# Second batch's z loaded earlier and turned in four pieces, unit 1's waiting squares put into feed-forward buffers, and a quarter of each diagonal block filled by a transpose instead of scores

## The chip, the cores and the metric

One core of a Trainium2 chip runs the whole kernel. The metric is the device time of one execution in microseconds (us); smaller is better. The kernel before was timed in 3 runs: 1248.04, 1248.33 and 1249.73 us, median 1248.33 us. The profile comes from one further execution, which has its own time of 1249.53 us.

The engines are called by short names: PE multiplies matrices (PEld is its loading of weights, which overlaps the multiplying), DVE and ACT are the two engines that can read PSUM and do elementwise work here, POOL does elementwise work in SBUF and issues some DMAs, and SP issues the other DMAs, strictly one after the other.

## What is computed

Two layers, one behind the other: a gated attention without softmax, and a feed-forward layer on its result.

```python
# u, v: (8, 3008, 256), z: (8, 3008, 64)
scores = (1/S) * (z @ z.T)              # per batch, S = 3008: symmetric
attn = maximum(scores, 0) ** 2          # symmetric as well
x = u * (attn @ v)
# x: (24064, 256), w_in: (256, 2048), w_out: (2048, 256)
h = x @ w_in
g = h * (1 / (1 + exp(-1.702 * h)))
out = g @ w_out                         # float32
```

The squared scores of a batch form a symmetric 3008 by 3008 matrix, since both factors of the product are the same z.

## The kernel before, in words

**Units and tiles.** A batch has 3008 rows, which are handled as 24 blocks of 128 (`NJ`; the last block has 64 rows, loaded twice). Query columns are taken 512 at a time: these are the *units*, `n` = 0 to 47, six to a batch (`NIS` = 6, `isup = n % 6`). For a unit, the keys are taken in pairs of blocks, `t` = 0 to 11; the pair `t` holds blocks `2t` and `2t+1`. One *score tile* `(n, t)` is made by `scores` (L250): two matmuls of 64 rows by 512 columns, which run side by side in the two halves of PE (L263), into a PSUM tile; a relu by ACT or DVE from PSUM to a float16 tile of 128 x 1024 (L292, L294); and a square in place (L278, L280). With `t // 2 == isup` the tile lies on the diagonal: its four key blocks are the unit's own four query blocks.

**Half of the matrix is transposed, not computed.** From unit 3 on, the tiles below the diagonal (`turned_from`, L186) are not computed: a tile of an earlier unit is transposed by a DMA that SP issues (`turn`, L231, L242) into one of 12 turned tiles `T`. The diagonal tiles are computed in full, in each unit two of them, `t = 2*isup` and `t = 2*isup + 1`. Tiles live in a ring of 14 buffers (`ap_`, `NA`), and `a_left` counts what still has to read one before its buffer is used again. In batch 0 nothing can be taken from a turned tile at first, so units 0 and 1 keep six tiles each outside the ring (`home`, L200): those of unit 0 in the not yet needed `V16[1]`, three of unit 1 in `ZT[1]` and three in `z16`.

**Values and feed-forward.** `values` (L391) multiplies the squares with `v` into four PSUM banks (L403: two matmuls of 64 rows by 256 columns side by side for each 128 x 128 block). At the end of a unit the banks are drained by ACT and DVE (L382, L384), summed and gated with `u` by POOL (L377, L419), transposed by SP (`turn_x`, L318, L325) into `XT` and copied with the halves exchanged into `XS` (`swap_x`, L336). The feed-forward layer takes 512 tokens `m` at a time, three units behind (`LAG`): `hidden` (L486, L493) makes one of 8 hidden tiles, ACT its sigmoid (L500), DVE the product `GT` (L504; 8 buffers, `NG`), and `outs` (L520, L531) multiplies with `w_out`.

**z of the next batch.** `load_z` (L105) is a DMA on POOL's queue into `z16`; `turn_z` (L116) copies all 24 blocks beside themselves on POOL (L118), and then SP transposes all of `z16` into `ZT[b % 2]` in one DMA (L119). `ZT` is the operand of all scores of batch `b`.

**What sets the order.** The order is worked out when the program is built, by a planner in the same file that keeps a clock for each engine (`now`) and adds a fixed cost for each operation (`cost`, L131). `work` (L556 to L577) is the fixed sequence on PE: the value steps `o` of unit `n`, then the output steps `y` of block `n - 3`. Between two steps, whenever a PSUM tile is free in the planner's clock, `filler` (L667) puts in a score tile or a hidden tile, the one that is due sooner. Elementwise operations go to the engine that ends first (`advance`, L152); DMAs of SP wait in `sends` and go out by their due number, lowest first, as soon as the planner's clock says that they are ready. Loads hang on steps of `work` (`at`, L593; L600 to L609): a step `(n, j)` is the first value step of unit `n` with key block `j`, and `hold` (L221) makes POOL wait for the newest square first. For the second batch (b = 1) z is loaded at (3, 8) and turned at (4, 0), later than in the other batches, because unit 1's squares sit in `ZT[1]` and `z16`; for the others at (n0+1, 13) and (n0+2, 13), where n0 is the first unit of the batch before. The filler counts z as there as soon as `turn_z` has been called (L115, L258, L673); it keeps no time for the transpose.

Of the kernel before, what the change touches and what calls it, by code (L numbers as in the profile page):

```python
# [9 lines left out]
F16 = mybir.dt.float16  # L10
P = 128
# [3 lines left out]
def kernel(  # L15
# [10 lines left out]
    AF = mybir.ActivationFunctionType  # L26
    ALU = mybir.AluOpType

    B, S, D = u.shape
    DQK = z.shape[2]  # L30
# [4 lines left out]
    ISUP = 512  # L35
    NIB = ISUP // P
    NIS = (S + ISUP - 1) // ISUP
    NP = NJ // 2
    NTOK = B * S
    TB = 512  # L40
# [4 lines left out]
    LAG = 3  # L45
    RING = (LAG + 1) * TB
    H = P // 2
    assert NTOK % TB == 0 and NJ == NIS * NIB and 2 * DQK == P and 2 * SREM == P and D == 2 * P and TB == ISUP

    CSC = 16.0  # L50
    FSC = CSC * CSC * float(S) * float(S)

    dve, act, pe, sp, pool = nc.vector, nc.scalar, nc.tensor, nc.sync, nc.gpsimd
# [3 lines left out]
    NG = 8  # L57
# [6 lines left out]
    pb = ctx.enter_context(tc.tile_pool(name="pb", bufs=2))  # L64
# [30 lines left out]
    VQ = 4  # L95
    VN = NJ // VQ
# [8 lines left out]
    def load_z(b):  # L105
        rows(b, z, 0, NJ, z16[:, :, 0, :], pool)
# [4 lines left out]
                f0 = e * DFF // 2 + c * D  # L111
                pool.dma_start(W1[e * H:(e + 1) * H, c, :, :], moe_w_in[:, f0:f0 + D].rearrange("(k p) f -> p k f", p=H))

    turned = {0}

    def turn_z(b):  # L116
        turned.add(b)
        pool.tensor_copy(z16[:, :, 1, :], z16[:, :, 0, :])  # L118
        sp.dma_start_transpose(ZT[b % 2], z16.rearrange("p n a d -> p (n a d)"))  # L119

# [7 lines left out]
    now = {"pe": 6.0, "act": 6.0, "dve": 7.0, "pool": 6.0, "sp": 6.0}  # L130
    cost = {  # L131
        ("act", "relu"): 1.03, ("dve", "relu"): 1.23, ("act", "sq"): 1.03, ("dve", "sq"): 0.7,
        ("act", "part"): 0.6, ("dve", "part"): 0.7, ("pool", "add"): 1.1, ("act", "sig"): 1.03, ("dve", "gt"): 1.23, ("pool", "gate"): 1.2,
        ("sp", "turn"): 1.45, ("sp", "turn_x"): 2.6, ("sp", "store"): 0.6, ("sp", "swap"): 1.2,
    }
    BOTH = ("act", "dve")
    FIRST = ("part", "gate", "add")
# [6 lines left out]
    def push(ready, kind, engines, fn):  # L144
        nonlocal pushed
        pushed += 1
        ops.append((ready, pushed, kind, engines, fn))

    def send(ready, kind, due, fn, ok=None):
        sends.append((ready, kind, due, fn, ok))  # L150

    def advance(t):  # L152

        while ops:
            best = None
            for o in ops:
                e = min(o[3], key=lambda x: max(now[x], o[0]) + cost[(x, o[2])])
                key = (max(now[e], o[0]), o[2] not in FIRST, o[2] == "sq", o[1])
                if best is None or key < best[0]:
                    best = key, o, e  # L160
            (start, *_), o, e = best
            if start > t:
                break
            ops.remove(o)
            now[e] = start + cost[(e, o[2])]
            o[4](e, now[e] + T_SEM)
        while now["sp"] <= t:
            can = [o for o in sends if o[0] <= t and (o[4] is None or o[4]())]
            if not can:
                break  # L170
            o = min(can, key=lambda o: (o[2], o[0]))
            sends.remove(o)
            now["sp"] = max(now["sp"], o[0]) + cost[("sp", o[1])]
            o[3](now["sp"])

    def pe_at(rows_, dur):
        if mode[0] != rows_:
            now["pe"] += T_SW
            mode[0] = rows_
        now["pe"] += dur  # L180
        return now["pe"] + T_LAT
# [4 lines left out]
    def turned_from(n, J):  # L186
        return n >= NDIR and J < n % NIS and (n, J) != (NDIR, NDIR - 1)

    def turns(n, t):

        return t // 2 > n % NIS and turned_from(n - n % NIS + t // 2, n % NIS)

    pairs = [(n, t) for n in range(NU) for t in range(NP) if not turned_from(n, t // 2)]
    nxt = 0


    def lend(x, k):
        return x[:, k * 2 * ISUP:(k + 1) * 2 * ISUP].rearrange("p (g c) -> p g c", g=2)

    home = {}  # L200
    for k in range(6):
        home[(0, 6 + k)] = lend(V16[1].rearrange("p n d -> p (n d)"), k)
        home[(1, 6 + k)] = lend(ZT[1].rearrange("p n d -> p (n d)") if k < 3 else z16.rearrange("p n a d -> p (n a d)"), k % 3)
    ring = []
    A, A_at, a_left = {}, {}, {}
    T, T_at, T_left, T_col = {}, {}, {}, {}
# [24 lines left out]
    def turn(n, t, at):  # L231

        b, isup = divmod(n, NIS)
        key = (b * NIS + t // 2, isup)
        if key not in T:
            c = colors.pop(0)
            T_col[key] = c
            T[key] = ptp.tile([P, NIB, NIB, P], F16, name=f"T{c}", tag=f"T{c}")
            T_left[key] = [2, NIB]
        a = A[(n, t)]  # L240
        g0 = (t % 2) * 2
        sp.dma_start_transpose(  # L242
            T[key][:, g0:g0 + 2, :, :].rearrange("p g i r -> p (g i) r"), a.rearrange("p g c -> p (g c)"),
        )
        T_left[key][0] -= 1
        if T_left[key][0] == 0:
            T_at[key] = at + T_DMA
        a_left[(n, t)] -= 1

    def scores(k):  # L250

        nonlocal nxt
        for i in range(k):
            n, t = pairs[nxt]
            nxt += 1
            b, isup = divmod(n, NIS)
            Z = ZT[b % 2]
            assert b in turned  # L258
            p_ = take_ps()
            sc = psA.tile([P, 2, ISUP], F32, name="sc", tag="A")  # L260
            for g in range(2):
                h0 = g * DQK
                pe.matmul(  # L263
                    sc[:, g, :], Z[h0:h0 + DQK, 2 * t + g, :],
                    Z[h0:h0 + DQK, isup * NIB:(isup + 1) * NIB, :],
                    start=True, stop=True,
                )
            if (n, t) in home:
                a = home[(n, t)]
            else:  # L270
                a = pap.tile([P, 2, ISUP], F16, name="ap_", tag="ap_")
                ring.append((n, t))
            A[(n, t)] = a
            a_left[(n, t)] = 2 + turns(n, t)

            def squared(e, at, n=n, t=t, a=a, isup=isup):
                if e == "act":
                    act.activation(a, a, AF.Square, scale=1.0)  # L278
                else:
                    dve.tensor_tensor(a, a, a, ALU.mult)  # L280
                if isup == NIS - 1 and t == NP - 1:
                    pool.memset(a[:, 1, ISUP - SREM:], 0.0)
                    at += 0.5
                A_at[(n, t)] = at
                latest[0] = a
                if turns(n, t):
                    key = (n - isup + t // 2, isup)
                    send(at, "turn", NDIR if n == 1 and (n, t) in home else key[0], lambda at: turn(n, t, at), lambda: key in T or len(colors) > 0)

            def relu(e, at, p_=p_, sc=sc, a=a, squared=squared):  # L290
                if e == "act":
                    act.activation(a, sc, AF.Relu, scale=CSC)  # L292
                else:
                    dve.tensor_scalar(a, sc, 0.0, CSC, ALU.max, ALU.mult)  # L294
                set_ps(p_, at)
                push(at, "sq", BOTH, squared)

            push(pe_at(H, T_SC), "relu", BOTH, relu)

    Os, Ys, GTs, Xs = {}, {}, {}, {}  # L300
    outs_done = 0
# [39 lines left out]
    def squares_of(n, j, ib):  # L341

        J = j // NIB
        if turned_from(n, J):
            return T[(n, J)][:, ib, j % NIB, :]
        return A[(n, j // 2)][:, j % 2, ib * P:(ib + 1) * P]

    def squares_at(n, j):

# [243 lines left out]
    def at(n, j, *fns):  # L593
        def go():
            hold()
            for f in fns:
                f()
        side[(n, j)] = go
# [4 lines left out]
    for b in range(1, B):  # L603
        n0 = (b - 1) * NIS
        late = b == 1
        at(n0 + 1 + 2 * late, 8 if late else 13, lambda b=b: load_z(b))
        at(n0 + 2 + 2 * late, 0 if late else 13, lambda b=b: turn_z(b))
        for q in range(VQ):
            at(n0 + 3 + late + q // 2, (EDGE + late, 12)[q % 2], lambda b=b, q=q: load_v(b, q))  # L609

# [56 lines left out]
    def filler():  # L667

        p_ = ps_free[ps_next % 2]
        if p_ is None or p_ > now["pe"]:  # L670
            return None
        can = []
        if nxt < len(pairs) and pairs[nxt][0] // NIS in turned and min(now["act"], now["dve"]) < now["pe"] + 0.8:  # L673
            old = len(ring) - NA
            if pairs[nxt] in home or old < 0 or not a_left[ring[old]]:
                can.append((urgent(("a",) + pairs[nxt], 3.0), "a"))
        if hnext < len(hids) and hnext - outs_done < NG and now["act"] < now["pe"] + 1.5 and now["dve"] < now["pe"] + 2.0:
            m = hids[hnext][0]
            xt = xt_at[m * TB // 64:(m + 1) * TB // 64]
            if None not in xt and max(xt) <= now["pe"] and (m or work[wi][1] >= LAG or work[wi][0] == "y"):  # L680
                can.append((urgent(("h",) + hids[hnext], 5.0), "h"))
        return min(can, default=None)

# [70 lines left out]
```

## Time and profile before

| what | value |
|---|---|
| median of 3 runs | 1248.33 us |
| profiled execution, its own time | 1249.53 us |
| its span (first to last instruction) | 1247.8 us |
| PE busy, matmuls | 1228.2 us, 18600 instructions |
| DVE, ACT, POOL busy | 937.7, 819.2, 472.9 us |
| SP's transposes of score tiles (L242) | 232 issues |
| transposes of z (L119) | 7 issues, median 4.195 us each on SP |
| copies of z on POOL (L118) | 7, 1454 ns each |
| HBM traffic | 60.29 MB read, 24.64 MB written |

How to read it: an engine's busy time is the union of its instructions. The page has the span in 40 slices, so a stall of a few microseconds shows only in queries with a window. A line such as `L263 PE MATMUL sc<-ZT 64*128 64x512 f16 x688` stands for all 688 matmuls of line 263 that write the tile `sc` from `ZT`, 64 rows by 512 columns. In lists of waits each entry is who waited, at which line, for whose result, the sum, the count and the longest. An arrow in brackets at the end of a line of a timeline tells how long the engine had been idle before it and what ended that. PEclk is the share of the full TensorE clock that the profile's clock rows show as granted in that stretch.

### The profile page before, as it was taken

What the parts mean: (1) busy time and instruction counts of PE and PEld (TensorE: products, weight loads), DVE (VectorE), ACT (ScalarE), POOL (GpSimd) and SP (SyncE); (2) the same over time, 40 slices, a digit from 0 to 9 for tenths busy, and PEclk for the clock granted to TensorE, in tenths of its full rate; (3) what the DMA queues carried; (4) which work ended last, traced back from release to release, by engine and by line L of the source; (5) the groups of instructions that cost most, each with busy time, mean ns of one, the idle gap of its engine ahead of it and who ended that gap; (6) DMA issues with size and microseconds to landing.
All of it is one profiled execution on the core that took longest, in us unless ns stands there. A gap on an engine that the chain in (4) does not pass through costs nothing.

```text
span 1247.8 us, 41921 instructions
## 1 busy us (share of the span) xinstructions
PE 1228.2 (98%) x18600; PEld 1012.1 (81%) x18600; DVE 937.7 (75%) x906; ACT 819.2 (66%) x933; POOL 472.9 (38%) x447
## 2 busy tenths in 40 slices
PE   8898999999999999999999999999999999999998
PEld 6786789989998877888778887788877888778886
DVE  8975877677888778876788768877687776877556
ACT  8765677666767657766667656676566665766444
POOL 5443343432434335343343424343343434322331
PEclk9998999999999999999999999999999999999999
DMA  9998796867987939788399684968659876575211
GB/s 158 176 175 144 142 133 133 149 113 124 135 148 148 147 90 137 145 151 150 85 137 154 131 144 95 134 126 166 131 102 149 158 126 117 113 144 104 67 45 60
DMA packets 442134, 161.74 MB, mean 130 GB/s; under 512 B 351840, under 2 KB 441952, under 8 KB 441952
## 3 DMA queue, kind: packets, MB, share of 16 engines
q1 hardware_dynamic: 390528, 141.62, 60.1%
q0 software_dynamic: 51424, 17.44, 14.5%
q8 instruction: 145, 2.38, 0.8%
q14 instruction: 37, 0.30, 0.1%
HBM read 60.29 MB, written 24.64 MB: 68 GB/s over the span
## 4 chain that ended last, share of the span: by engine, by line
PE 93%; DVE 5%; DMA 1%; issue 1%; ACT 0%; DVEq 0%; ACTq 0%
PE O L403 36%; PE hg L493 25%; PE yps L531 25%; PE sc L263 6%; PE O L478 1%; DMA ZT<-z 1%; PE O L465 1%; DVE GT L504 1%; PE warm L625 0%; DVE sums L384 0%; DVE ap__8058 L280 0%; DVE ap__2897 L280 0%; PE ztp L634 0%; DVE ap__1020 L280 0%; DVE ap__1039 L280 0%
## 5 line engine op out<-in xcount | busy, mean ns | idle before, releaser
L504 DVE TENSOR_TENSOR GT<-hg,tsg 128x1024 f16<-128x1024 f32 x376 | 456.8, 1221 | 212.0 <-ACT tsg L500 210.6
L500 ACT ACTIVATE tsg<-hg 128x1024 f16<-128x1024 f32 x376 | 381.1, 1024 | 275.1 <-PE hg L493 248.6
L377 POOL TENSOR_TENSOR sums<-sums 128x512 f32<-128x512 f32 x188 | 249.3, 1327 | 666.6 <-ACT sums L382 349.5
L493 PE MATMUL hg<-XT,W 64*128 64x512 f16 x1504 | 387.9, 376 | 3.0 <-DVE GT L504 1.9
L531 PE MATMUL yps<-W,GT 64*128 64x256 f16 x6016 | 374.7, 270 | 1.2 <-DVE GT L504 0.9
L493 PE MATMUL hg<-XS,W 64*128 64x512 f16 x1504 | 370.3, 376 | 0.0
L531 PEld LDWEIGHTS <-GT 64*128 64x128 f16 x6016 | 324.5, 94 | 47.9 <-issue 1.5
L493 PEld LDWEIGHTS <-W 64*128 64x128 f16 x3008 | 175.9, 94 | 87.5 <-issue 6.0
L403 PE MATMUL O<-V,T 64*128 64x256 f16 x3392 | 217.4, 269 | 0.1
L403 PEld LDWEIGHTS <-T 64*128 64x128 f16 x3392 | 185.9, 94 | 28.0 <-issue 0.3
L419 POOL TENSOR_TENSOR X<-sums,RU 128x512 f16<-128x512 f32 (+2 forms) x104 | 140.6, 1353 | 7.8
L263 PE MATMUL sc<-ZT 64*128 64x512 f16 x688 | 126.2, 379 | 9.3 <-DMA ZT<-z 4.3
L382 ACT ACTIVATE sums<-O 128x512 f32<-128x512 f32 x114 | 65.3, 596 | 52.6 <-PE O L403 46.7
L384 DVE TENSOR_SCALAR sums<-O 128x512 f32<-128x512 f32 x78 | 52.9, 687 | 33.8 <-PE O L403 30.1
L382 ACT ACTIVATE sums<-yps 128x512 f32<-128x512 f32 x111 | 63.8, 592 | 17.1 <-PE yps L531 15.9
L384 DVE TENSOR_SCALAR sums<-yps 128x512 f32<-128x512 f32 x73 | 50.0, 685 | 14.1 <-issue 9.9
L263 PEld LDWEIGHTS <-ZT 64*128 64x128 f16 x688 | 40.2, 94 | 16.0 <-issue 6.4
L87 POOL DMA_DIRECT2D V<-in_v_dram x32 | 28.1, 878 | 0.0
L87 POOL DMA_DIRECT2D z<-in_z_dram x7 | 11.0, 1566 | 0.4 <-issue 0.4
L478 PE MATMUL O<-V,T 128*64 128x256 f16 x160 | 10.3, 275 | 0.0
L118 POOL COPY z<-z 128x1536 f16<-128x1536 f16 x7 | 10.2, 1454 | 0.0
L478 PEld LDWEIGHTS <-T 128*64 128x64 f16 x160 | 8.1, 110 | 1.9 <-issue 1.9
(1538 smaller groups left out, 1522.5 us busy)
## 6 DMA issues: line engine op xcount, KB each, us to landing
out_dram<-sums SPq DMA_DIRECT2D x92, 256.0 KB, 4.1
RU<-in_u_dram SPq DMA_DIRECT2D x40, 512.0 KB, 4.7
V<-in_v_dram POOLq DMA_DIRECT2D x24, 384.0 KB, 6.8
XS<-XT SPq DMA_DIRECT2D x60, 128.0 KB, 3.8
RU<-in_u_dram SPq DMA_DIRECT2D x8, 384.0 KB, 3.8
z<-in_z_dram POOLq DMA_DIRECT2D x7, 368.0 KB, 9.3
V<-in_v_dram POOLq DMA_DIRECT2D x8, 320.0 KB, 8.8
XT<-X SPq DMA_TRANSPOSE x144, 2.5
```

Source lines behind the costliest of these rows:

```text
L87: eng.dma_start(dst[:, :full - lo, :], dram[b, lo * P:full * P].rearrange("(n p) d -> p n d", p=P),)
L263: pe.matmul(sc[:, g, :], Z[h0:h0 + DQK, 2 * t + g, :], Z[h0:h0 + DQK, isup * NIB:(isup + 1) * NIB, :], start=True, stop=True,)
L377: pool.tensor_tensor(s_[:, 0, :, :], s_[:, 0, :, :], s_[:, 1, :, :], ALU.add)
L382: act.activation(s_[:, g, :, :], ps[g], AF.Copy, scale=scale)
L384: dve.tensor_scalar(s_[:, g, :, :], ps[g], scale, None, ALU.mult)
L403: pe.matmul(O[g][:, i2, :], half(sq, g), half(V[:, j, :], g), start=(j == 0 and i2 == 0), stop=(ends and j == js[-1] and (i2 == 1 or short)),)
L419: pool.tensor_tensor(X[:p, :, ib:ib + k, :].rearrange("p c n d -> p n c d"), both[:p, ib - 2 * h:ib - 2 * h + k, :].rearrange("p n (c d) - ...
L478: pe.matmul(O[c0:c0 + SREM, 1, :], squares_of(n, j, NIB - 1)[:, :SREM], V[:, j, :], start=False, stop=False, tile_position=(0, c0),)
L493: pe.matmul(hg[:, e, :], half(W1[:, fg // 2, c, fg % 2 * P:(fg % 2 + 1) * P], e), half(x[:, c // 2, p0:p0 + TB], e), start=(c == 0), stop= ...
L500: act.activation(tsg, hg, AF.Sigmoid, scale=1.702 / FSC)
L504: dve.tensor_tensor(GT, hg, tsg, ALU.mult)
L531: pe.matmul(Y[g][:, i2, :], half(GT[:, e, s * P:(s + 1) * P], g), half(W2[:, ff, :], g), start=(fg == 0 and e == 0 and i2 == 0), stop=(end ...
```

## The change

Three edits, made together.

1. **z of the second batch.** The six tiles that unit 1 keeps outside the ring move from `ZT[1]` and `z16` into six of the eight `GT` buffers. A hidden tile that would use such a buffer is held back until the tile in it has been read and transposed (`lent` in `filler`). z of batch 1 is loaded at (2, 14) in place of (3, 8).
2. **Turning z in pieces.** For every batch `turn_z` does a quarter at a time: a copy of six blocks on POOL and a transpose of six blocks on SP, at (3, 14), (3, 16), (3, 18), (3, 20) for batch 1 in place of (4, 0), and at (n0+2, 6), (n0+2, 8), (n0+2, 10), (n0+2, 12) for the others in place of (n0+2, 13). The transpose goes through `sends` with the due number of the third unit before the batch, and the planner books 2.2 us of SP for each. The filler asks for scores of a batch only when the planner's time for the last quarter has come (`z_at`).
3. **A quarter of each diagonal block.** From the second batch on (`NMIR` = 6, 42 units), the second diagonal tile `t = 2*isup + 1` computes only its right half: 2 matmuls of 256 columns, and a relu and a square of 128 x 512 in place of 128 x 1024. Its left half is filled by a DMA transpose that SP issues (`mirror`, 128 x 512) from the right half of the first diagonal tile, once that is squared. The two diagonal tiles are laid out by column halves (`by_halves`), so that source and destination are each one run. The planner counts the tile as ready when both its square and 3.5 us behind the mirror's issue have passed.

```diff
                 pool.dma_start(W1[e * H:(e + 1) * H, c, :, :], moe_w_in[:, f0:f0 + D].rearrange("(k p) f -> p k f", p=H))
-    turned = {0}
-    def turn_z(b):
-        turned.add(b)
-        pool.tensor_copy(z16[:, :, 1, :], z16[:, :, 0, :])
-        sp.dma_start_transpose(ZT[b % 2], z16.rearrange("p n a d -> p (n a d)"))
+    z_at = {0: 0.0}
+    def turn_z(b, q):
+        c = slice(q * VN, (q + 1) * VN)
+        pool.tensor_copy(z16[:, c, 1, :], z16[:, c, 0, :])
+        def turn(at):
+            sp.dma_start_transpose(ZT[b % 2][:, c, :], z16[:, c, :, :].rearrange("p n a d -> p (n a d)"))
+            if q == VQ - 1:
+                z_at[b] = at + T_DMA
+        send(now["pe"] + 1.0, "turn_z", b * NIS - 3, turn)
...
         ("act", "relu"): 1.03, ("dve", "relu"): 1.23, ("act", "sq"): 1.03, ("dve", "sq"): 0.7,
+        ("act", "relu_half"): 0.6, ("dve", "relu_half"): 0.7, ("act", "sq_half"): 0.6, ("dve", "sq_half"): 0.42,
         ("act", "part"): 0.6, ("dve", "part"): 0.7, ("pool", "add"): 1.1, ("act", "sig"): 1.03, ("dve", "gt"): 1.23, ("pool", "gate"): 1.2,
-        ("sp", "turn"): 1.45, ("sp", "turn_x"): 2.6, ("sp", "store"): 0.6, ("sp", "swap"): 1.2,
+        ("sp", "turn"): 1.45, ("sp", "mirror"): 1.3, ("sp", "turn_x"): 2.6, ("sp", "turn_z"): 2.2, ("sp", "store"): 0.6, ("sp", "swap"): 1.2,
     }
...
                 e = min(o[3], key=lambda x: max(now[x], o[0]) + cost[(x, o[2])])
-                key = (max(now[e], o[0]), o[2] not in FIRST, o[2] == "sq", o[1])
+                key = (max(now[e], o[0]), o[2] not in FIRST, o[2][:2] == "sq", o[1])
                 if best is None or key < best[0]:
...
         return t // 2 > n % NIS and turned_from(n - n % NIS + t // 2, n % NIS)
+    NMIR = NIS
+    def mirrored(n, t):
+        return n >= NMIR and t == n % NIS * 2 + 1
     pairs = [(n, t) for n in range(NU) for t in range(NP) if not turned_from(n, t // 2)]
...
         home[(0, 6 + k)] = lend(V16[1].rearrange("p n d -> p (n d)"), k)
-        home[(1, 6 + k)] = lend(ZT[1].rearrange("p n d -> p (n d)") if k < 3 else z16.rearrange("p n a d -> p (n a d)"), k % 3)
+        home[(1, 6 + k)] = pb.tile([P, 2, TB], F16, name="GT", tag="GT", bufs=NG)
     ring = []
...
         a_left[(n, t)] -= 1
+    def by_halves(a):
+        return a.rearrange("p g c -> p (g c)").rearrange("p (i g c) -> p g i c", i=2, g=2)
+    def mirror(n, at):
+        t = n % NIS * 2
+        sp.dma_start_transpose(
+            A[(n, t + 1)].rearrange("p g (i r) -> p (g i) r", i=NIB)[:, :NIB, :],
+            A[(n, t)].rearrange("p g c -> p (g c)")[:, ISUP:],
+        )
+        a_left[(n, t)] -= 1
+        half_at(n, at + T_DMA)
+    halves_at = {}
+    def half_at(n, at):
+        halves_at.setdefault(n, []).append(at)
+        if len(halves_at[n]) == 2:
+            A_at[(n, n % NIS * 2 + 1)] = max(halves_at[n])
     def scores(k):
...
             Z = ZT[b % 2]
-            assert b in turned
+            assert b in z_at
             p_ = take_ps()
             sc = psA.tile([P, 2, ISUP], F32, name="sc", tag="A")
+            low = NIB // 2 if mirrored(n, t) else 0
+            cols = slice(low * P, ISUP)
             for g in range(2):
...
                 pe.matmul(
-                    sc[:, g, :], Z[h0:h0 + DQK, 2 * t + g, :],
-                    Z[h0:h0 + DQK, isup * NIB:(isup + 1) * NIB, :],
+                    sc[:, g, cols], Z[h0:h0 + DQK, 2 * t + g, :],
+                    Z[h0:h0 + DQK, isup * NIB + low:(isup + 1) * NIB, :],
                     start=True, stop=True,
                 )
+            part = "_half" if low else ""
             if (n, t) in home:
...
             A[(n, t)] = a
-            a_left[(n, t)] = 2 + turns(n, t)
-            def squared(e, at, n=n, t=t, a=a, isup=isup):
+            a_left[(n, t)] = 2 + (turns(n, t) or mirrored(n, t + 1))
+            def squared(e, at, n=n, t=t, a=a, isup=isup, cols=cols):
+                x = by_halves(a)[:, :, 1, :] if mirrored(n, t) else a
                 if e == "act":
-                    act.activation(a, a, AF.Square, scale=1.0)
+                    act.activation(x, x, AF.Square, scale=1.0)
                 else:
-                    dve.tensor_tensor(a, a, a, ALU.mult)
+                    dve.tensor_tensor(x, x, x, ALU.mult)
                 if isup == NIS - 1 and t == NP - 1:
...
                     at += 0.5
-                A_at[(n, t)] = at
+                if mirrored(n, t):
+                    half_at(n, at)
+                else:
+                    A_at[(n, t)] = at
+                    if mirrored(n, t + 1):
+                        send(at, "mirror", n - 1, lambda at: mirror(n, at), lambda: (n, t + 1) in A)
                 latest[0] = a
...
                     send(at, "turn", NDIR if n == 1 and (n, t) in home else key[0], lambda at: turn(n, t, at), lambda: key in T or len(colors) > 0)
-            def relu(e, at, p_=p_, sc=sc, a=a, squared=squared):
+            def relu(e, at, p_=p_, x=sc, y=a, part=part, squared=squared):
                 if e == "act":
-                    act.activation(a, sc, AF.Relu, scale=CSC)
+                    act.activation(y, x, AF.Relu, scale=CSC)
                 else:
-                    dve.tensor_scalar(a, sc, 0.0, CSC, ALU.max, ALU.mult)
+                    dve.tensor_scalar(y, x, 0.0, CSC, ALU.max, ALU.mult)
                 set_ps(p_, at)
-                push(at, "sq", BOTH, squared)
-            push(pe_at(H, T_SC), "relu", BOTH, relu)
+                push(at, "sq" + part, BOTH, squared)
+            if low:
+                relu.__defaults__ = (p_, sc[:, :, cols], by_halves(a)[:, :, 1, :], part, squared)
+            elif mirrored(n, t + 1):
+                relu.__defaults__ = (p_, sc.rearrange("p g (i c) -> p g i c", i=2), by_halves(a), part, squared)
+            push(pe_at(H, T_MM if low else T_SC), "relu" + part, BOTH, relu)
     Os, Ys, GTs, Xs = {}, {}, {}, {}
...
             return T[(n, J)][:, ib, j % NIB, :]
-        return A[(n, j // 2)][:, j % 2, ib * P:(ib + 1) * P]
+        a = A[(n, j // 2)]
+        if mirrored(n, j // 2) and ib < NIB // 2:
+            return a[:, 0, (2 * ib + j % 2) * P:(2 * ib + j % 2 + 1) * P]
+        if J == n % NIS and n >= NMIR:
+            return by_halves(a)[:, j % 2, ib // 2, ib % 2 * P:(ib % 2 + 1) * P]
+        return a[:, j % 2, ib * P:(ib + 1) * P]
     def squares_at(n, j):
...
         late = b == 1
-        at(n0 + 1 + 2 * late, 8 if late else 13, lambda b=b: load_z(b))
-        at(n0 + 2 + 2 * late, 0 if late else 13, lambda b=b: turn_z(b))
+        at(*((n0 + 2, 14) if late else (n0 + 1, 13)), lambda b=b: load_z(b))
+        for q in range(VQ):
+            at(n0 + 2 + late, (14 if late else 6) + 2 * q, lambda b=b, q=q: turn_z(b, q))
         for q in range(VQ):
...
         can = []
-        if nxt < len(pairs) and pairs[nxt][0] // NIS in turned and min(now["act"], now["dve"]) < now["pe"] + 0.8:
+        if nxt < len(pairs) and z_at.get(pairs[nxt][0] // NIS, now["pe"] + 1.0) <= now["pe"] and min(now["act"], now["dve"]) < now["pe"] + 0.8:
             old = len(ring) - NA
...
             xt = xt_at[m * TB // 64:(m + 1) * TB // 64]
-            if None not in xt and max(xt) <= now["pe"] and (m or work[wi][1] >= LAG or work[wi][0] == "y"):
+            lent = hnext - (NG - 6)
+            if None not in xt and max(xt) <= now["pe"] and not (0 <= lent < 6 and a_left[(1, 6 + lent)]) and (m or work[wi][1] >= LAG or work[wi][0] == "y"):
                 can.append((urgent(("h",) + hids[hnext], 5.0), "h"))
```

## The prediction before the result was known

> **What bounds the kernel now.** I read the page's busy times and the chain of work that ended last, then PE's waits, then the windows, and at last the timeline around the longest wait.
>
> ```profile
> PE 1228.2 (98%) x18600; PEld 1012.1 (81%) x18600; DVE 937.7 (75%) x906; ACT 819.2 (66%) x933; POOL 472.9 (38%) x447
> ...
> PE 93%; DVE 5%; DMA 1%; issue 1%; ACT 0%; DVEq 0%; ACTq 0%
> ```
>
> PE is busy for 98% and 93% of the chain are PE's own matmuls. So time leaves the span in two ways only: fewer or shorter matmuls, or fewer holes on PE. PE's waits over the whole span, and then windows (columns: us from the start, length, busy time and count of PE, PEld, DVE, ACT, POOL, granted PE clock, DMA share, GB/s):
>
> ```profile
> PE sc L263 <- DMA ZT<-z: 4.3, 1, 4.3
> PE hg L493 <- DVE GT L504: 1.9, 2, 1.5
> PE sc L263 <- DVE ap__826 L294: 1.6, 1, 1.6
> PE sc L263 <- DVE ap__490 L294: 1.4, 1, 1.4
> ```
> ```profile
> 99.18:103.49 4.31, 0.00 (x0) 0.00 (x0) 0.00 (x0) 1.02 (x1) 2.38 (x2) 0.81 1.25 235
> 103.49:108.67 5.18, 5.18 (x44) 3.17 (x46) 2.93 (x3) 2.23 (x3) 2.38 (x3) 0.50 0.39 115
> ```
> ```profile
> 400.00:600.00 200.00, 199.57 (x3042) 160.59 (x3039) 150.88 (x145) 130.03 (x150) 77.69 (x72) 1.00 0.81 134
> 600.00:800.00 200.00, 199.96 (x3057) 157.43 (x3055) 153.59 (x148) 133.57 (x153) 75.96 (x71) 1.00 0.76 131
> ```
>
> From 400 us on there are no holes left to win (199.96 of 200 us). The largest hole is the wait of 4.32 us at 99.18 for z of the second batch; behind it PE runs for 5.18 us at a clock of 0.50. The timeline shows why: SP comes to the transpose only at 93.35, is kept by it for 8.11 us, and the data lands 10.1 us after the issue, while the planner keeps no time for it.
>
> ```profile
> 93.35 8.11 SPq L119 DMA_TRANSPOSE ZT<-z  x1
> ...
> 98.78 0.40 PE L263 MATMUL sc<-ZT 64*128 64x512 f16 x2
> ...
> 103.49 0.61 PE L263 MATMUL sc<-ZT 64*128 64x512 f16 x2 [4.32 <-DMA ZT<-z]
> ```
>
> **Edit 1 and 2 for batch 1: the stall goes, -6.9 us.** The hole is 4.32 us. At half clock 5.18 us hold 2.59 us of work, so 2.59 us more are lost: 6.9 us together. Does z come in time? Key block 14 of unit 2 is at about 49 us (by counting the weight loads of L403), where the load was at 61.1 us. Its landing took up to 10.2 us, so z16 is full by about 61. The four copies hang on steps of unit 3 at about 66 to 69 us. On SP one issue of 1024 columns takes at least 1.23 us (L242) and one of 3072 columns 3.56 us (L119), so a piece of 768 takes about 0.9 us and four 3.6; even at the 8.1 us of the crowded case plus the 10.1 us of its landing, z is there by about 87 us, 12 us before the scores that waited. What SP queues behind the pieces: transposes of batch 0's tiles for unit 4. They have room: the tightest turned tile of all lands 14.9 us before its first use (unit 4, J = 3, used at 92.8 us), and the tightest from unit 6 on 22.9 us. What is late next? At 104 us the output steps follow, whose GT tiles DVE had ended by 98.3 us, and the banks were drained by ACT 0.6 us after the O matmuls; so nothing else stands at that place.
>
> Of the clock the Trainium skill (TensorE: Matmul & The Clock Gate, "What's actually happening") says that it halves after an idle window of about 3.4 us and comes back after about as long busy. The row shows 5.18 us of half clock after the restart; by the page 3.4 us, a loss of 1.7 in place of 2.59 us, and the stall would be an estimated 6.0 us. The measured 6.9 stands.
>
> **Edit 1, its price at the front: +0.5 us.** The load of z now runs about 50 to 60 us, among W2's end, unit 1's transposes and XS for the first hidden tile. That XS landed 3.6 us before its use at 56.0 us (issued at 48.3 and 49.0, landing 3.3 and 3.6 us later). Beside the old load of z the same copy took 7.1 and 7.4 us. From below 0 (XS ahead of the load), even a gain of up to 1.5 us (the wait at 60.07 us for GT falls differently); from above 3.8 us later, of which 3.6 are slack, plus the same for a tile behind it: 2 us. I take 0.5. The GT buffers lent to unit 1 cost nothing: its squares were read by about 40 us, their transposes landed by 59.3 us, and the first hidden tile is at 56.0 us; only the third and later ones need such a buffer.
>
> **Edit 2 for the other batches: 0.** Seven copies of 1454 ns become 28 of about 364, and 21 more `hold` copies of 0.18 us come in: 4 us of POOL, which idles 62%. SP issues the same columns; no PE wait of these six batches was for z. The cover is the distance between the copy and the first scores of the next batch, 20 us or more; nobody waits on it.
>
> **Edit 3: a quarter of the diagonal, -4.5 us.** In the chain in order of time, 16 matmuls of 512 columns take 1.73 us and 32 of 256 columns 1.75 us:
>
> ```profile
> 75.03 1.75 PE yps L531 x32
> ...
> 82.66 1.73 PE hg L493 x16
> ```
>
> Two run side by side, so a pair costs 0.216 and 0.109 us. Each of the 42 units trades one pair for the shorter: 42 x 0.107 = 4.5 us, all of it on the path, as PE has no holes there. ACT and DVE give up half of 84 operations (1.03 and 1.22 us for a relu, 0.7 to 1.75 for a square, about 45 us in all), worth nothing by itself, as neither is the bound.
>
> What the edit adds is a wait: the first value step that reads the second diagonal tile waits for the mirror, and behind it stands all of PE. How long before its use is the source ready? For the second tile of unit 8, the tightest of the 42:
>
> ```profile
> L403 PEld LDWEIGHTS <-ap__3459 x16: 94/94/94, 200.3 to 202.9; 64*128 64x128 f16 x16
> ...
> L280 DVE TENSOR_TENSOR ap__3459<-ap__3459 x1: 865/865/865, 187.8 to 187.8; 128x1024 f16<-128x1024 f16 x1
> ```
>
> This tile is squared at 188.7 and read at 200.3 us. The first tile of the unit, from which the mirror is made, is squared at 184.8 (its ACT row starts at 183.7 and takes 1.05 us): 15.5 us before the need. Worked out alike for the other units, the lead is 16.4 us in unit 7, 18 to 34 us in the others up to unit 15, and 37 us or more from unit 16 on. Against that: an issue of about 0.6 us (half of 1.23), and 3.0 to 8.9 us from issue to landing, as L242's tiles show at 150 to 200 us. So 0 on PE. From above, an SP held up for its longest wait (16.1 us, L318 for X) would eat it in the early units; I keep that for the rivals. SP gets 42 x 0.6 = 25 us more, on 785 us of issues; the DMA engines 42 x 128 KB = 5.5 MB more on 161.7 MB.
>
> **The planner's new order: 0, between -2 and +2 us.** With other costs and due numbers all later steps are dealt out anew. The small holes between 131 and 425 us sum up to 2.0 us; they may go or come again.
>
> **Sum.** Against the profiled execution: 1249.53 - 6.9 - 4.5 + 0.5 = 1238.6 us. That execution is 1.2 us above the median of 1248.33, so for a median: **1237.4 us**.
>
> **Rivals.**
> (A) The stall moves and does not go: the scores of batch 1 come on time, but SP, now with pieces ahead of turn_x and the score tiles in the busiest stretch (DMA share 2.52 at 65 to 70 us, queued packets), delivers XT or a turned tile late, and PE stops elsewhere between 75 and 140 us. For it: the 4.3 us of SP's L242 issue at 66.7 us. Against: the slack of 14.9 us, and the old load leaves that stretch. Price: half to all of the 6.9 us comes back: 1241 to 1244.5 us.
> (B) Change without effect: the mirror's saving is eaten, because the dealt-out order leaves holes of 0.1 us a unit, and A holds too: 1246 to 1250.8.
> (C) Slower: the mirror is late in PE's queue. SP works strictly in order; if it stands for its longest wait of 16.1 us in front of a mirror that then takes the longest landing of L242 behind 40 us (11.9 us, the issue at 89.0 us), the data comes 28 us after the square. In unit 8 that is 12.5 us after the need, in unit 7 11.6, and a hole of over 4 us brings half clock behind it, 2.6 us: 15.1 and 14.2 us. The gain of 10.9 us is gone from a mirror that lands 23.8 us after its square in unit 8 (15.5 + 10.9 - 2.6); with one such event it is 1252.5 us, with both 1267. For it: the early leads, and PE's strict order. Against: SP's long waits arise where SP has run ahead of its work, not where it is behind, and a mirror goes out by a low due number.
> A shorter remainder of the z stall belongs to A; holes of up to 1.65 us kept the clock at 1.00 here, so it would cost its length alone. The Trainium skill (same page and section) agrees: less than one window idle does not halve the clock.
>
> **How the numbers follow.** The forecast, 1234 to 1241 us, has 0.64: its lower end is all of 11.4 us and the 2 us of small holes, its upper end the 2 us of the front and 2 us of new holes. A 0.15, B 0.09, C 0.12 (1251 and more). No more than 2 in 10 is to be left out, so the range reaches through A: 1234 to 1245 us. 0.2% is 2.5 us, about what a measurement of this kernel can tell from no change: faster (below 1245.8) 0.79, same 0.09, slower 0.12.
>
> **What would show it.** Right: no PE wait for ZT, a clock of 1.00 from 10 us to the end, L263 with 84 matmuls of 256 columns and PE's busy time down by about 4.5 us plus the 2.6 of the half clock; 42 mirrors on SP; no PE wait for a DMA. Wrong: a PE wait for a DMA from `ap_` (C), for T, XS or XT between 60 and 140 us (A), or holes spread thinly over all units (B).

## The result and the profile after

The changed kernel takes 1241.04 us (median of 4 runs, 1240.06 to 1242.39) against 1248.18 us for the kernel before (4 runs): the medians differ by 7.1 us, and the measured ratio of 0.9947, 95% interval 0.9934 to 0.9959, is some 6.6 us. The time lies inside the range of the prediction and on its side, 3.6 us above the 1237.4 that was named. The profiled execution took 1240.06 us against 1249.53 before; it is the fastest of the four, and the last experiment below shows a second execution of it, with half clock, which this one lacks.

The page of the changed kernel, its busy times:

```profile
PE 1219.2 (98%) x18600; PEld 1018.0 (82%) x18600; DVE 908.7 (73%) x891; ACT 810.3 (65%) x948; POOL 476.0 (38%) x489
```

PE is busy for 9.0 us less with the same number of instructions. The scores by shape (busy us and mean ns, then the idle time before them):

```profile
L301 PE MATMUL sc<-ZT 64*128 64x512 f16 x604 | 116.5, 376 | 5.4 <-DVE ap__832 L339 1.7 <-DVE ap__496 L339 1.4 <-DVE GT L339 0.4
...
L301 PE MATMUL sc<-ZT 64*128 64x256 f16 x84 | 12.3, 269 | 0.0
```

84 matmuls have become 256 columns long, and no score waits for ZT any more. But PE's list of waits has a new first line, and the list of ACT's waits between 95 and 112 us says what lies behind it:

```profile
PE yps L585 <- ACT sums L436: 3.7, 1, 3.7
PE hg L547 <- DVE GT L558: 2.0, 2, 1.5
```
```profile
ACT sums L436 <- DMA out_dram<-sums: 4.5, 1, 4.5
```

The timeline of the changed kernel from 100 us, with rows of SP's queue ahead of it:

```profile
82.47 2.42 SPq L385 DMA_DIRECT2D XS<-XT  x2
84.93 5.74 SPq L122 DMA_TRANSPOSE ZT<-z  x3
90.80 3.85 SPq L367 DMA_TRANSPOSE XT<-X  x2
...
100.26 1.95 SPq L602 DMA_DIRECT2D out_dram<-sums  x2
```
```profile
104.31 0.60 ACT L436 ACTIVATE sums<-O 128x512 f32<-128x512 f32 x1 [4.53 <-DMA out_dram<-sums]
...
104.95 0.27 PE L585 MATMUL yps<-W,GT 64*128 64x256 f16 x1 [3.73 <-ACT sums L436]
```

So this is the chain: PE has finished the value sums of unit 4 and wants the two PSUM banks back for its output steps. ACT and DVE, which drain the banks, need a `sums` buffer, and there are three. The first output block's two sums sit in two of them, added up by POOL at 83.1 and 84.5 us (a row of L431 at 81.69, two operations in 2.79 us), but SP issues their stores only at 100.26 us and behind, and the first lands at 104.2 (3.9 us after its issue). In the kernel before, z's transpose landed at 103.4 and the same store, issued at 101.52, at about 104.2 (2.6 to 2.7 us after the issue):

```profile
101.52 1.08 SPq L548 DMA_DIRECT2D out_dram<-sums  x2
...
104.61 0.60 ACT L382 ACTIVATE sums<-O 128x512 f32<-128x512 f32 x1 [4.38 <-PE O L403]
```

The two waits end within a microsecond of each other. The change removed the one that was seen, and the other, which it had hidden, took its place.

The store is not late for its due number, which is the lowest, 1 (`m + 1`). The planner's own clock puts its issue at 78.9 us; SP comes to it some 21 us behind that plan, with everything that the plan has ahead of it still in the queue. A part of that backlog is older than this stretch: the six transposes of unit 1's squares (L256, out of `GT`, between 37.6 and 57.7 us) keep SP for 1.3 to 5.7 us each, 2.9 in the median, where the planner books 1.45.

### The profile page after: what moved, and what is told of

It reads as the page before. It is cut to its first block, busy times and chain, and to the rows that moved or that the text cites. A ratio compares the mean times of both kernels' runs of the same rounds, so it can differ in the third digit from the quotient of the medians.

```text
span 1238.1 us, 42078 instructions
## 1 busy us (share of the span) xinstructions
PE 1219.2 (98%) x18600; PEld 1018.0 (82%) x18600; DVE 908.7 (73%) x891; ACT 810.3 (65%) x948; POOL 476.0 (38%) x489
## 4 chain that ended last, share of the span: by engine, by line
PE 88%; DVE 1%; ACT 1%; issue 1%; DVEq 0%
PE O L457 33%; PE hg L547 25%; PE yps L585 24%; PE sc L301 4%; PE O L532 1%; PE O L519 1%; DVE GT L558 0%; DVE ap__6020 L320 0%; DVE ap__18204 L320 0%; DVE ap__12112 L320 0%; DVE sums L438 0%; DVE ap__21289 L339 0%; DVE ap__3546 L339 0%; DVE ap__9105 L339 0%; DVE ap__15197 L339 0%
## 5 line engine op out<-in xcount | busy, mean ns | idle before, releaser
L431 POOL TENSOR_TENSOR sums<-sums 128x512 f32<-128x512 f32 x188 | 248.7, 1325 | 681.2 <-DVE sums L438 431.1
L547 PE MATMUL hg<-XT,W 64*128 64x512 f16 x1504 | 383.5, 376 | 2.3 <-DVE GT L558 2.0
L585 PE MATMUL yps<-W,GT 64*128 64x256 f16 x6016 | 380.8, 269 | 4.7 <-ACT sums L436 3.7
L301 PE MATMUL sc<-ZT 64*128 64x512 f16 (+1 forms) x688 | 122.3, 363 | 5.4 <-DVE ap__832 L339 1.7
L438 DVE TENSOR_SCALAR sums<-O 128x512 f32<-128x512 f32 x82 | 55.6, 685 | 20.6 <-issue 9.9
L438 DVE TENSOR_SCALAR sums<-yps 128x512 f32<-128x512 f32 x69 | 47.4, 687 | 14.7 <-issue 10.1
L119 POOL COPY z<-z 128x384 f16<-128x384 f16 x28 | 13.8, 493 | 0.0
```

What stands on the lines that cost most here:

```text
L301: pe.matmul(sc[:, g, cols], Z[h0:h0 + DQK, 2 * t + g, :], Z[h0:h0 + DQK, isup * NIB + low:(isup + 1) * NIB, :], start=True, stop=True,)
L431: pool.tensor_tensor(s_[:, 0, :, :], s_[:, 0, :, :], s_[:, 1, :, :], ALU.add)
L438: dve.tensor_scalar(s_[:, g, :, :], ps[g], scale, None, ALU.mult)
L547: pe.matmul(hg[:, e, :], half(W1[:, fg // 2, c, fg % 2 * P:(fg % 2 + 1) * P], e), half(x[:, c // 2, p0:p0 + TB], e), start=(c == 0), stop= ...
L585: pe.matmul(Y[g][:, i2, :], half(GT[:, e, s * P:(s + 1) * P], g), half(W2[:, ff, :], g), start=(fg == 0 and e == 0 and i2 == 0), stop=(end ...
```

## The experiments

Each kernel was timed beside the kernel before on the same chip.

**A fourth sums buffer in the changed kernel.**

```diff
-        s_ = pb.tile([P, 2, 2, D], F32, name="sums", tag="sums", bufs=3)
+        s_ = pb.tile([P, 2, 2, D], F32, name="sums", tag="sums", bufs=4)
...
-        o = pb.tile([P, 2, 2, D], F32, name="sums", tag="sums", bufs=3)
+        o = pb.tile([P, 2, 2, D], F32, name="sums", tag="sums", bufs=4)
```

> The changed kernel with a fourth buffer for the tile 'sums' and nothing else. Theory (the stall moved to a buffer): the hole of 3.73 us at 101 us is ACT and DVE waiting for one of three sums buffers, which an output store of SP still reads; with a fourth buffer the hole is gone and nothing of like size stands behind it: 1241.0 - 3.7 = 1237.3 us, no hole over 2 us on PE between 90 and 140 us. Rival (SP's backlog): what is late is all that SP delivers in this stretch, the buffer is only the first of it; the hole comes back within 20 us at an XT, XS or T that has not landed: 1239.5 to 1241 us.

Measured: 1236.08 us (1235.83 to 1236.35), ratio to before 0.991 (0.9896 to 0.9924). The windows of its trace (columns as in the prediction) show PE idle for 0.26 us in these 30, where a hole of 3.73 us had been:

```profile
90.00:100.00 10.00, 10.00 (x160) 8.47 (x156) 7.29 (x7) 5.74 (x7) 1.26 (x1) 1.00 1.42 187
100.00:110.00 10.00, 9.74 (x148) 7.80 (x144) 9.37 (x11) 6.61 (x8) 5.40 (x5) 1.00 0.89 173
110.00:120.00 10.00, 10.00 (x156) 8.24 (x152) 6.53 (x6) 6.09 (x7) 4.63 (x8) 1.00 1.15 214
```

The theory of the moved stall holds, the rival of a general backlog falls: with the buffer PE waits for nothing else here. The gain against the changed kernel is some 5 us, more than the 3.7 us of the hole that the theory had counted (1237.3 us). The two profiled executions, neither with half clock at this place, differ by just 3.8 us in span (1238.1 and 1234.3). Half clock, which comes with the hole in other executions, as the last experiment shows, is the likely rest.

**Each part of the change alone.** In `e_mirror` the kernel before gets only edit 3; in `e_nomirror` the changed kernel loses it:

```diff
-    NMIR = NIS
+    NMIR = NU
```

> The kernel before with edit 3 alone (the quarter of each diagonal block filled by a transpose); z and unit 1's squares as before. Theory: a pair of 512 columns becomes a pair of 256 in 42 units, 4.5 us, and the z stall of 4.3 us with its half clock stays: 1248.2 - 4.5 = 1243.7 us. Rival (the mirrors cost part of it in waits or in SP's queue): 1245 to 1248 us.

> The changed kernel without edit 3 (all diagonal tiles computed in full), edits 1 and 2 kept. Theory: of the z stall's 6.9 us the new hole gives back 3.7, so 1248.2 - 3 = 1245.3 us, that is 4.5 us above the changed kernel, and the hole of some 3.7 us before the outputs is there as well. Rival (the mirrors make the new hole, as one goes out in this stretch): no hole there, 1241 to 1242 us.

Measured: edit 3 alone 1240.4 us (1238.22 to 1243.43; ratio 0.9946, interval 0.993 to 0.9961); edits 1 and 2 alone 1247.17 us (1245.08 to 1249.69; ratio 0.9999, interval 0.999 to 1.0009), beside 1247.76 for the kernel before in the same set of runs. Both expectations missed: edit 3 gave 7.4 us and not 4.5, and the earlier z gave nothing that can be measured, not 3. So edit 3 alone is as fast as the whole change (1240.4 beside 1241.04 us). The 7.4 us are blurred: the runs of that kernel spread over 5 us, and its hole was shorter by 1.2 us in the profiled execution. A cleaner value follows below. First lines of PE's waits in edit 3 alone, and then in edits 1 and 2 alone:

```profile
PE sc L294 <- DMA ZT<-z: 3.1, 1, 3.1
```
```profile
PE yps L585 <- ACT sums L436: 4.6, 1, 4.6
```

With edits 1 and 2 alone the wait for z is gone and the wait for sums is longer than the 4.32 us that went. The rival for that kernel (the mirrors make the new hole) falls: it is there without them.

**A fourth buffer in the kernel before.** The same edit as above, on the kernel before.

> The kernel before with a fourth sums buffer and nothing else. Theory (two waits beside each other): the store that frees the buffer lands at 104.1 us in the profile of before, 0.6 us behind the end of the z stall, so the wait for z hides it, and a buffer more changes nothing while z is late: 1247.5 to 1248.2 us. Rival (the buffers alone bound the front): 1244 to 1245 us.

Measured: 1246.78 us (1243.86 to 1248.71), ratio 0.9996 (0.9986 to 1.0006), no change that can be told from the 1247.76 us of the kernel before. The median lies 0.7 us below the range that the theory gave, and 1.8 us above the rival's. Its PE waits for z as ever:

```profile
PE sc L263 <- DMA ZT<-z: 3.9, 1, 3.9
```

**Both waits removed, without edit 3.** Edits 1 and 2 and the fourth buffer.

> Edits 1 and 2 without edit 3, and a fourth sums buffer. Theory (two waits side by side, each hiding the other): early z alone gave 0.6 us and the fourth buffer alone 1.0 us against the kernel before, together they take the whole stall: some 6.6 us above the changed kernel with four buffers (1236.1), so 1242.0 to 1243.0 us, and no hole over 1 us between 90 and 140 us. Rival (the buffer pays only where the mirrors have freed SP and DVE): 1245 us or more.

Measured: 1241.43 us (1241.0 to 1241.8), ratio 0.9949 (0.9935 to 0.9962), beside 1247.45 for the kernel before. The theory had 1242.0 to 1243.0, so the gain is a little larger than expected. The four cases of the front are: before 1247.8, z early 1247.2, one more buffer 1246.8, both 1241.4 (the last from the set of runs with 1247.45 for the kernel before). Neither is worth a measurable amount by itself, and both together are worth 6.0 us. Against the four-buffer version with edit 3 (1236.08, from another set of runs whose kernel before was 0.3 us slower) edit 3 is worth about 5.4 us here, where no stall blurs it: 5.4 us by the medians and by the spans of the two profiles (1239.7 and 1234.3 us), 5.7 when each is taken from its own kernel before, 4.9 by the two ratios. Counted from start to start, the 84 short matmuls take 54.6 ns each, and the long ones in the steady part 108: 84 x 53.4 ns = 4.5 us, as predicted. Summed from each matmul's start to the next one's over the two traces, the scores take 4.5 us less, and of the rest 0.9 us less follows on hidden matmuls, while the value and output steps agree within 0.2 us. The planner also places the score and hidden tiles anew, and no run shows whether the 0.9 us come from that.

**Is it the order on SP, or are the DMA engines full?** In the changed kernel with its three buffers, the first block's two stores are issued from POOL.

```diff
-                    sp.dma_start(out.rearrange("(n p) c -> p n c", p=P)[:, r0:r0 + 2, :], s_)
+                    (sp if m else pool).dma_start(out.rearrange("(n p) c -> p n c", p=P)[:, r0:r0 + 2, :], s_)
                     stored.add((m, h))
 
+                if m == 0:
+                    store(at)
+                    return
                 send(at, "store", m + 1, store)
```

> The changed kernel, three sums buffers; only the two output stores of the first token block are issued from POOL's queue as soon as their sum is there, in place of waiting in SP's. Theory (the order on SP holds the store): the sums are there at about 85 us, a POOL load issued then lands 7 to 10 us later, so the buffer is free by 96 us and the hole at 101 us goes: 1236 to 1237 us. Rival (the DMA engines are full in this stretch, share 1.0 to 1.4): the store lands as late as before from any queue, the hole stays over 2 us: 1239 to 1241 us.

Measured: 1235.89 us (1235.5 to 1236.31), ratio 0.9905 (0.9891 to 0.9918): as good as the fourth buffer, without its memory. POOL's queue, from its timeline, and the landing of the two stores:

```profile
83.79 0.79 POOL L602 DMA_DIRECT2D out_dram<-sums  x1 [0.30 <-POOL sums L431]
...
86.18 0.74 POOL L602 DMA_DIRECT2D out_dram<-sums  x1 [0.30 <-POOL sums L431]
```
```profile
DMA to landing us min/median/max: 3.1/4.0/4.9
```

In this crowded stretch the store lands in 3.1 to 4.9 us when it is issued at once. What held it was some 16 us in SP's strict order behind transposes and loads, not the DMA engines. The expectation had it land in 7 to 10 us, and was too careful there. The Trainium skill (DMA: Bandwidth & Descriptors, "Issuing engines are not separate DMA queues") says that all issuing engines share the same 16 DMA engines and that issuing from several saves only the sequencer's time, which is usually small. The landings fit the first half, as the store takes about as long from POOL as from SP (3.9 to 4.1 us). The second half does not fit: what the store waits for in SP's one queue, behind the issues of other transfers, was the whole 5 us here.

**One piece or four.** The four-buffer version with z turned in one piece.

```diff
-        c = slice(q * VN, (q + 1) * VN)
+        c = slice(0, NJ)
...
-        for q in range(VQ):
-            at(n0 + 2 + late, (14 if late else 6) + 2 * q, lambda b=b, q=q: turn_z(b, q))
+        at(n0 + 2 + late, 20 if late else 12, lambda b=b: turn_z(b, VQ - 1))
```

> The changed kernel with four sums buffers, z of each batch turned in one piece in place of four (for the second batch at the last of the four places, step 20 of unit 3; for the others at step 12), booked with 4.2 us of SP. Theory (the earlier time counts, the pieces do not): z is still there before 98 us, no hole comes, 1235.8 to 1236.8 us. Rival (one transpose of 3072 columns keeps SP for up to 8 us, as in the kernel before, and what stands behind it comes late): a hole of over 2 us between 90 and 140 us, or 0.3 us more in each of the later batches: 1238 us or more.

Measured: 1236.22 us (1235.42 to 1236.48), the same as in four pieces. Of edit 2 only the earlier time counts.

**The mirror where its lead is short.** The four-buffer version with edit 3 from unit 3 on (`NMIR = 3`).

> The changed kernel with four sums buffers and edit 3 from unit 3 on (45 units in place of 42). Theory: 3 x 0.107 us, and half of three relus and squares in a stretch where DVE is the bound: 1235.3 to 1235.9 us. Rival: in units 3 to 5 SP is behind (17 us behind its plan), the mirrors land late and PE waits: 1237 us or more.

Measured: 1243.58 us (1242.71 to 1244.2), 7.5 us slower than with edit 3 from unit 6 on; the theory missed, the rival came. The mirror of unit 3, in the timeline, and the step that reads it:

```profile
66.04 1.26 SPq L385 DMA_DIRECT2D XS<-XT  x2
67.40 1.31 SPq L256 DMA_TRANSPOSE T<-ap__886  x1
68.76 1.27 SPq L271 DMA_TRANSPOSE ap__1006<-ap__983  x1
```
```profile
71.43 0.83 PE L457 MATMUL O<-V,ap__1006 64*128 64x256 f16 x12 [4.43 <-DMA ap__1006<-ap__983]
```

The mirror's source is squared at 54.8 us, SP comes to the mirror at 68.76; PE wants its data at 67.0 and stands for 4.43 us. By the clock rows 3.4 us at half clock follow, a loss of 1.7, so 6.1 of the 7.5 us are seen in this execution. This is rival C of the prediction, in the one place where the lead is too short for SP's backlog: in the kernel before, the first of these tiles was squared 13 us ahead of the use of the second. From unit 6 on no PE wait for a mirror appears in any of the profiles.

**The changed kernel once more, for its spread.**

> The changed kernel once more, for its spread and a second profile. Theory (the clock gate makes the spread): a hole of 3.7 to 4.6 us halves the clock in some executions and not in others, in steps of 3.4 us of half clock, so its runs spread over 2 us or more (1239 to 1243), whereas the version with four buffers, which has no such hole, spread over 0.5 us. Rival (the spread is of the chip): as narrow as the four-buffer version or just shifted.

Measured: 1241.32 us (1239.98 to 1243.05; ratio 0.9949, interval 0.9937 to 0.9962), the spread that was expected. Windows over the hole and behind it, first of the profiled execution of the changed kernel, then of this one (columns as before; the clock is the third number from the right):

```profile
101.22:104.95 3.73, 0.00 (x0) 0.00 (x0) 0.62 (x2) 0.64 (x2) 0.00 (x0) 1.00 1.19 238
104.95:112.00 7.05, 6.60 (x91) 5.13 (x92) 6.61 (x7) 4.19 (x5) 2.76 (x3) 1.00 0.30 61
```
```profile
101.53:105.99 4.46, 0.00 (x1) 0.00 (x0) 0.63 (x2) 0.65 (x2) 0.00 (x0) 0.79 1.12 238
105.99:110.96 4.97, 4.97 (x32) 3.74 (x33) 4.52 (x6) 2.83 (x3) 2.76 (x3) 0.50 0.25 60
```

The same hole, 0.7 us longer, brings 4.97 us at half clock with it, so 2.5 us of loss; the profiled execution that came with the result had none. That is very likely why it was the fastest of its four runs. The kernels with a hole of 3 to 5 us here spread over 1.5 to 5.2 us, those without one over 0.5 to 1.1 us. Half clock is a part of that spread and perhaps not all of it: of 23 runs of the kernel before, the five with a mean granted clock of 1.0 took 1244.56 to 1246.06 us and the four with 0.996 took 1248.78 to 1249.12, but those with 0.999 lie anywhere between 1245.4 and 1249.17.

## Why the prediction was right, and where it was not

- **The total** was 1237.4 and came out at 1241.0. That is what rival A gave (1241 to 1244.5), not the forecast: "the stall moves and does not go". Its mechanism was right in kind, its place was not: not XT or a turned tile, but the store of the first output block. That the time still lies in the stated range is no merit of the forecast's sum. The range reaches through A, one of the two large terms came and the other did not.
- **The step that failed** is "What is late next? [...] so nothing else stands at that place". The prediction took from ACT's draining at 104.61 us that the banks were free for the asking. It did not ask what ACT's target was waiting for. The row was there: SP's store at 101.52 us in the kernel before, with three buffers for a tile that value sums and output sums share. ACT's list named PE as its releaser, because that came last, by some 0.4 us.
- **The term of -6.9 us for the stall** is somewhat high even as the worth of removing the whole stall: 6.0 us with both waits gone (1247.45 to 1241.43). It was read from an execution of 1249.53 us, slower than 37 of the 41 later runs of the kernel before, with a long stretch at half clock. As the worth of edits 1 and 2 it is 0, within 0.1% of the time.
- **z in time** came true, with far less room than the prediction gave. The four copies end at 64.1 us, but SP, behind its work, comes to the pieces only between 81.14 and 88.6 us, and the last lands 8.8 us later, at 97.4, not "by about 87". The first scores of batch 1 start at 98.5.
- **The diagonal, -4.5 us**: right in its mechanism, and a little low: about 5.4 us where nothing blurs it, of which 4.5 are the shorter matmuls. The mirror adds no wait from unit 6 on, as its leads said.
- **The front, +0.5 us**: nothing. The holes at the start stand as they were; the DVE wait of 1.5 us before the first hidden tiles is the same in both lists of waits.
- **SP's prices** were too low: a mirror of 512 columns takes 1.2 us to issue, not 0.6, and a quarter of z 1.23 us in the quiet case, not 0.9 (on POOL, a quarter's copy 492 ns, not 364). The mirrors did not reach PE. Three pieces of z stand with 5.74 us in SP's queue ahead of the late store, as the whole z stood there with 8.11 us before; what they alone add to the hole no run separates.
- **B** did not come: the mirror's saving is there in full. **C** did not come in the change, and came in the test that took its lead away.
- Of what "would show it", the clock of 1.00 (but for the last 2 us) and the missing wait for ZT came true in the profile, and a hole of 3.73 us remained all the same: they are signs of one wait gone, not of time gained.

## What to carry to other kernels

When a wait is about to be removed, list everything that becomes free or lands within a few microseconds of its end, buffers on the far side of a store included; the list of waits names the last one only, and a removal is worth the distance to the next. Two waits that end together can be worth nothing one by one and everything as a pair, as here, so test them as a pair. In an in-order DMA queue a small store with a tight deadline does not belong behind long transfers. A due number in a planner did not keep it ahead of them here, since the real queue ran some 21 us behind the planner's clock; another queue did.

## What the runs showed of the hardware

- The clock: idle times of 3.13 us (edit 3 alone) and 4.46 us (the second profile of the changed kernel) led to half clock, one of 3.73 us did not. In the kernel before with four buffers, 3.89 us idle were followed by 1.34 us at full clock and then 3.40 at half:

```profile
99.10:102.99 3.89, 0.01 (x2) 0.01 (x2) 0.00 (x0) 1.02 (x1) 2.38 (x2) 1.00 1.23 254
102.99:104.33 1.34, 1.34 (x24) 1.10 (x26) 0.91 (x1) 0.64 (x2) 0.00 (x0) 1.00 1.06 325
104.34:107.74 3.40, 3.40 (x34) 2.15 (x30) 2.85 (x4) 2.41 (x3) 2.37 (x3) 0.50 0.16 44
```

  Of this the Trainium skill (TensorE: Matmul & The Clock Gate, "What's actually happening") says that activity is judged in windows of 3413 ns that run freely. The stretches at half clock here, 3.40 us in this run and 6.83 us in the profile of the kernel before (5.18 us behind the hole, and 1.65 us of the hole itself by its mean clock of 0.81), are one and two of these. The clock rows of the other traces have the same two lengths: 6.83 us for edit 3 alone, for edits 1 and 2 alone and for the second profile of the changed kernel, 3.41 us for `e_sums4_nmir3`. The length of the hole does not decide between them: 3.13 us brought two, 4.43 us one, 3.73 us none. So a hole of that size has no fixed price: its length, and 0 to 3 us on top.
- The rule in the prediction that less than one window idle does not halve the clock, for which it names the Trainium skill, did not hold here: 3.13 us are less than 3413 ns, and the mean clock of 0.84 in that hole puts the drop some 2.1 us behind PE's last matmul (by its modelled end). The measurement decides, for holes of 3 us and more; holes of up to 1.7 us kept the clock at 1.00 here.

```profile
99.10:102.23 3.13, 0.00 (x0) 0.00 (x0) 0.00 (x0) 1.02 (x1) 2.37 (x2) 0.84 1.12 277
102.23:108.05 5.82, 5.82 (x52) 3.79 (x54) 3.78 (x4) 2.56 (x3) 2.64 (x3) 0.50 0.34 101
```

- A DMA transpose of 512, 768 and of 1024 columns takes SP the same 1.2 us to issue when nothing presses (1.22, 1.23, 1.23), one of 3072 columns 3.56 us. Cutting z into four pieces makes 4.9 us of 3.56.
